# Feed-forward part: two passes over halves of the inner dimension, six token tiles a block, GpSimd's work on VectorE

## The chip, the cores and the metric

One core of a Trainium2 chip. A core has TensorE (PE, the matmuls), VectorE (DVE), ScalarE (ACT), GpSimd (POOL) and SyncE (SP), which here issues the DMAs; each takes its instructions in the order in which they stand in its queue. The metric is the device time in microseconds (us), lower is better.

## The reference

Local attention feeds a soft mixture of experts, and that feeds a gated feed-forward part:

```python
x = attention(q, k, v)                    # (2304, 512), 8 heads, window 32, plain or dilated
logits = x @ phi                          # 32 slots: 8 experts x 4
d = softmax(logits over tokens); slot_input = d.T @ x
slot_out = relu(slot_input @ w1[e]) @ w2[e]      # 8 experts, inner dimension 1024
x = softmax(logits over slots) @ slot_out        # c @ slot_out
h = x @ w_in                              # (2304, 2048)
g = h * sigmoid(h)                        # silu
out = g @ w_out                           # (2304, 512)
```

w_in (512 x 2048) and w_out (2048 x 512) arrive as 64-bit floats, all else as 32-bit ones.

## The kernel before

The kernel is a list of operations: `op(name, engine, cost, deps, fn)` records one, with an estimated cost and with what it must come after. `list_schedule` (line 885) puts all of them in one order: each engine takes, of those that are ready by the estimated times, the one with the longest estimated way to the end behind it, with small bonuses by kind (`PRIO`). The engines' queues follow that order, so the order within a queue is fixed beforehand. `mm` (line 78) records every matmul, so all matmuls have line 79.

The first 160 us are attention, the two softmaxes and the experts, with their weights streamed. Then comes the feed-forward part, from line 503 on. Because c has 32 columns only, A = slot_out @ w_in (32 x 2048) is formed first and h = c @ A afterwards. The inner dimension of 2048 is taken in 16 pieces of 128, called f; the 2304 tokens in 18 tiles of 128, called t. All products are exact to two parts: a value is split into a rounded high part and the rest.

For each f these are made:

- `cvi` (line 561, three DVE instructions at lines 539, 541 and 543) turns 64-bit w_in into 32-bit, `aq` (582) multiplies it into a piece of A in a PSUM bank, `ah` on ACT and `al` on DVE split that, and eight or four small ACT copies `ac` (618) put it in its place `astk`. One conversion of 512 columns is half of what two f need of w_in.
- `cvo` (568) turns one f of w_out into 32-bit, again three DVE instructions; `wh` (line 576, ACT) makes its high part, `wl` (663, GpSimd) subtracts that and leaves the rest. The four places of `wt` hold a raw w_out piece until its `wl` is done.
- `h` is the matmul of A's piece with c (transposed, in `ct`), into bank 6 or 7; ACT's silu (`si`, line 714) writes its result to `gtm`; `gh` is its high part, in the first group a second ACT pass over the bank (720), later a DVE cast (722); `gl` the rest (727), on GpSimd in the first group, on DVE later.
- `om` adds gh x wh, gh x wl and gl x wh for one f and one tile into the tile's bank: three matmuls of 512 columns.

The tokens come in five groups of 5, 4, 4, 3 and 2 tiles. The first group goes f by f, as w_in and w_out are converted, with all five tiles open in five banks; its h comes in two parts, 256 and 384 columns wide. The other groups go tile by tile, with all 16 f of a tile in a row, from g values that are kept in the places where weights had been (`ring`). Each tile's bank is copied out once (`oe`, DVE and ACT in turn) and stored. The last tile goes in two halves of 256 columns.

Of the kernel before, what the change touches and what calls it, by code (L numbers as in the profile page):

```python
# [29 lines left out]
def fused_kernel(ctx: ExitStack, tc: tile.TileContext, a: dict):  # L30
# [5 lines left out]
    # ---- constants and small persistent tiles  # L36
# [26 lines left out]
    # ---- places that several tiles use one after the other: a new tile in a place begins once  # L63
    # every use of the one before it has been emitted
# [16 lines left out]
    # ---- a list of operations, each on one engine, with what it must come after; they are  # L81
    # put in an order by a small list scheduler, and emitted in that order
# [11 lines left out]
    # ================= attention =================  # L94
# [52 lines left out]
    def scores(m):  # L147
# [6 lines left out]
        # the plain heads' masks are the dilated ones' second block over and over, but for the first  # L154
# [136 lines left out]
    # ---- dispatch: softmax over tokens, kept as a running one over the four batches  # L291
# [6 lines left out]
    # what the batches so far have summed to is kept relative to their maximum  # L298
# [23 lines left out]
    # ---- combine: softmax over slots, transposed, in two exact parts  # L322
# [74 lines left out]
    # ---- token sums of the four batches put together, scaled, transposed  # L397
# [30 lines left out]
    # ---- experts, their weights streamed  # L428
# [78 lines left out]
    WIS = (("w10", "", ""), ("w11",), ("xk",), ("xq",), ("w10", "w11"), ("xk", "xq"))  # L507
    WIG = ((0, 2, 3, 4), (0, 4), (0, 4), (0, 4), (0, 2, 4), (0, 2, 4))
    WIC = ((0, 2), (2, 4), (4, 6), (6, 8), (8, 12), (12, 16))
    WIF = (("w12", 0), ("w12", 1024), ("xu", 0), ("xu", 1024), ("w12", 0), ("xu", 0))  # L510
    WOS = ("w13", "w14", "xp")

    def wi(q, k):
        w = 256 * (WIC[q][1] - WIC[q][0])
        if q == 0:
            return reg("wi0", w * WIG[0][k], w * (WIG[0][k + 1] - WIG[0][k]))
        return reg(f"wi{q}.{k}", 0, 2048)

# [13 lines left out]
    # the 32-bit form of a 64-bit float: sign and top exponent bit, the low seven bits of the  # L532
    # exponent and the mantissa's top 23
# [20 lines left out]
    def wif(q):  # L554
        place, o = WIF[q]
        key = f"wif{q - (o > 0)}"
        if key not in tiles:
            new(place, key)
        return reg(key, o, 512 * (WIC[q][1] - WIC[q][0]))

    def cvi(q, k, i):
        if q == 0:
            o, n = (0, 512, 768)[k], (512, 256, 256)[k]
            conv(wi(0, k), wif(0)[:, o:o + n], i)
        else:
            conv(wi(q, k // 2)[:, 1024 * (k % 2):1024 * (k % 2) + 1024], wif(q)[:, 512 * k:512 * k + 512], i)
# [6 lines left out]
    def whc(f):  # L573
        if f % 2 == 0:
            new(f"w{f // 2}", f"ws{f // 2}", F32R)
        act.copy(out=wh(f), in_=wt(f))  # L576

    def arow(q):
        f0, f1 = WIC[q]
        return slice(32 * (f0 % 4), 32 * (f0 % 4 + f1 - f0))  # L580

    def aq(q):
        f0, f1 = WIC[q]
        n = f1 - f0
        w = wif(q).rearrange("p (g f) -> p g f", g=4)
        for g in range(4):
            for s in range(n):
                r = 32 * ((f0 + s) % 4)
                mm(bank[4][r:r + 32, 384:512], sot[:, 32 * g:32 * g + 32], w[:, g, 128 * s:128 * s + 128], g == 0, g == 3)

    def ahc(q):
        act.copy(out=aqh[arow(q)], in_=bank[4][arow(q), 384:512])

    def alc(q):
        dve.tensor_tensor(out=aql[arow(q)], in0=bank[4][arow(q), 384:512], in1=aqh[arow(q)], op=ALU.subtract)
# [418 lines left out]
```

## Time and profile before

| | us |
|---|---|
| median of 3 runs | 416.8 (414.83 to 419.25) |
| the profiled execution, span | 416.7 |
| PE busy | 373.5 |
| DVE busy | 250.6 |
| ACT busy | 168.9 |
| GpSimd busy | 101.4 |

The span runs from the first to the last instruction. Busy times are sums over the whole span, so an engine that fills one stage and rests in another shows a middling share. A digit of the slices is the busy share of a fortieth of the span (10.4 us) in tenths.

### The profile page before, as it was taken

The numbers are of one execution on the slowest core, as the hardware profiler recorded it, in microseconds if no ns is written. First come the engines' busy times: TensorE is split into PE (matmuls) and PEld (weight loads), VectorE is DVE, ScalarE is ACT, GpSimd is POOL, SyncE is SP. The second block draws the span as 40 slices with busy tenths as digits, with TensorE's granted clock in tenths as the row PEclk, the third lists the DMA queues.
The fourth block names the chain that finished last, engine by engine and source line by source line (L and its number), as shares of the span: only waits on it lengthen the run. The fifth ranks groups of instructions, "written<-read, shape, count | busy, mean of one in ns | idle before, by whom it ended". The sixth has DMA issues, their size and how long they took to land.

```text
span 416.7 us, 8042 instructions
## 1 busy us (share of the span) xinstructions
PE 373.5 (90%) x3042; PEld 287.9 (69%) x3042; DVE 250.6 (60%) x614; ACT 168.9 (41%) x596; POOL 101.4 (24%) x118
## 2 busy tenths in 40 slices
PE   4797987998989998778786999999999999999997
PEld 3676766877862345546564678888888888888886
DVE  5888988888652028999999807900294004900730
ACT  2585655675521125455555856400252002400510
POOL 4314221221222013576928881000000000000000
PEclk9898998999999999989969899999999999999999
DMA  8999999997998999967320002020001000010000
GB/s 229 265 338 330 288 302 296 312 324 240 353 352 301 386 387 397 401 253 272 131 102 0 1 2 76 2 76 25 27 0 51 27 8 18 2 50 27 25 25 27
DMA packets 33080, 70.04 MB, mean 168 GB/s; under 512 B 2705, under 2 KB 3217, under 8 KB 33041
## 3 DMA queue, kind: packets, MB, share of 16 engines
q1 hardware_dynamic: 33040, 69.53, 49.8%
q8 instruction: 24, 0.39, 0.4%
q14 instruction: 16, 0.12, 0.1%
HBM read 64.80 MB, written 4.72 MB: 167 GB/s over the span
## 4 chain that ended last, share of the span: by engine, by line
PE 55%; DVE 25%; DMA 10%; ACT 3%; issue 2%; SPq 2%; POOL 1%; POOLq 0%; ACTq 0%; DVEq 0%
PE bank L79 55%; DMA w_w2.15_1839<-in_w 3%; ACT xp_pq L178 2%; DVE xu_wif L541 2%; DMA w_w1.2_342<-in_w 2%; DMA xp_pq<-in_q 2%; DVE xu_wif L543 2%; DVE xt_wt L541 2%; DVE xt_wt L543 2%; DVE w_wif L541 2%; DVE xt_pt L203 2%; DVE xt_pt L202 2%; DMA xv_v<-in_v 2%; DVE xt_pt L205 2%; DMA xk_k<-in_k 1%
## 5 line engine op out<-in xcount | busy, mean ns | idle before, releaser
L79 PE MATMUL bank<-w_ws,w_g 128*128 128x512 f32 (+1 forms) x318 | 75.1, 379 | 0.0
L714 ACT ACTIVATE xv_gtm<-bank 128x256 f32<-128x256 f32 (+2 forms) x96 | 46.7, 492 | 54.8 <-PE bank L79 52.7
L79 PEld LDWEIGHTS bank<-w_ws,w_g 128*128 128x128 f32 x318 | 56.8, 188 | 11.1
L178 ACT ACTIVATE xp_pq<-bank,stats 128x64 f32<-128x64 f32 x144 | 43.7, 337 | 29.7 <-DVE stats L170 23.8
L79 PE MATMUL bank<-w_ws,x_gz 128*128 128x512 f32 x165 | 46.6, 420 | 1.1 <-POOL w_ws L663 0.4
L191 POOL TENSOR_TENSOR xp_pq<-xp_pq,stats 128x320 f32<-128x320 f32 (+1 forms) x32 | 21.7, 678 | 74.8 <-ACT xp_pq L178 31.7
L79 PEld LDWEIGHTS bank<-w_ws,x_gz 128*128 128x128 f32 x165 | 32.2, 201 | 10.0 <-POOL x_gz L727 1.4
L663 POOL TENSOR_TENSOR w_ws<-xt_wt,w_ws 128x512 fp32r<-128x512 f32 x16 | 27.4, 1715 | 23.5 <-ACT w_ws L576 17.8
L79 PE MATMUL bank<-xk_k,xq_qp 128*64 128x64 f32 x576 | 25.8, 239 | 7.9 <-DVE xq_qp L144 7.8
L178 ACT ACTIVATION_READ_ACCUMULATOR xp_pq<-bank,stats 128x1 f32 x144 | 32.8, 228 | 0.0
L79 PE MATMUL bank<-ct_ct,w_astk 128*128 128x256 f32 (+2 forms) x96 | 31.9, 342 | 0.6 <-ACT w_astk L622 0.4
L809 DVE COPY w_ost<-bank 128x512 f32<-128x512 f32 x9 | 6.1, 686 | 41.7 <-PE bank L79 41.7
L79 PEld LDWEIGHTS bank<-xk_k,xq_qp 128*64 128x64 f32 x576 | 21.2, 148 | 14.2 <-DVE xq_qp L144 10.0
L79 PE MATMUL bank<-ip,xu_v2x 128*128 128x160 f32 x160 | 28.3, 316 | 1.7 <-DVE lg L262 1.5
L79 PE MATMUL bank<-xt_pt,xv_v 128*64 128x96 f32 (+1 forms) x396 | 23.6, 274 | 5.2 <-POOL xp_pq L191 2.1
L808 ACT COPY w_ost<-bank 128x512 f32<-128x512 f32 x8 | 4.7, 588 | 55.0 <-PE bank L79 54.8
L79 PEld LDWEIGHTS bank<-xt_pt,xv_v 128*64 128x64 f32 x396 | 21.2, 158 | 8.0 <-POOL xp_pq L191 2.2
L727 POOL TENSOR_TENSOR x_gz<-xv_gtm,x_gz 128x256 fp32r<-128x256 f32 (+1 forms) x22 | 25.2, 1161 | 1.9 <-ACT xv_gtm L714 1.9
L79 PEld LDWEIGHTS bank<-ip,xu_v2x 128*128 128x128 f32 x160 | 22.4, 189 | 4.2 <-DVE lg L262 1.6
L722 DVE CAST w_g<-xv_gtm 128x512 fp32r<-128x512 f32 (+2 forms) x30 | 11.7, 390 | 20.2 <-ACT xv_gtm L714 19.8
L79 PEld LDWEIGHTS bank<-ct_ct,w_astk 128*128 128x128 f32 x96 | 18.0, 189 | 5.8 <-ACT w_astk L622 1.3
L79 PE MATMUL bank<-w_ws,w_gy 128*128 128x512 f32 x75 | 21.1, 420 | 0.9 <-POOL w_gy L727 0.9
(222 smaller groups left out, 652.8 us busy)
## 6 DMA issues: line engine op xcount, KB each, us to landing
w_wo<-in_w_out SPq DMA_DIRECT2D x5, 1024.0 KB, 8.4
xp_pq<-in_q SPq DMA_DIRECT2D x16, 288.0 KB, 7.2
xk_k<-in_k SPq DMA_DIRECT2D x16, 288.0 KB, 7.0
out<-w_ost SPq DMA_DIRECT2D x17, 256.0 KB, 2.0
xv_v<-in_v SPq DMA_DIRECT2D x44, 72.0 KB, 6.2
xp_wo<-in_w_out SPq DMA_DIRECT2D x2, 1024.0 KB, 9.6
xu_v2x<-in_v SPq DMA_DIRECT2D x20, 72.0 KB, 5.9
w_w1.0_136<-in_w SPq DMA_DIRECT2D x1, 1024.0 KB, 8.5
```

The costliest lines, as they stand in the source:

```text
L79: pe.matmul(out, lhsT=lhsT, rhs=rhs, start=start, stop=stop, skip_group_check=True)
L178: act.activation(out=preg(n)[:, j0 + i, :], in_=bank[m % 3][:, 64 * i:64 * i + 64], func=ACTF.Exp, bias=nmx[:, r, i:i + 1], accum_out=sums ...
L191: pool.tensor_tensor(out=p, in0=p, in1=rinv[:, m % 4, 0:nj].rearrange("p (j o) -> p j o", o=1).to_broadcast([128, nj, 64]), op=ALU.mult)
L202: dve.transpose(out=t[0:64, j0:j1, 32:64], in_=p[64:128, j0:j1, 0:32])
L203: dve.transpose(out=t[64:128, j0:j1, 32:64], in_=p[64:128, j0:j1, 32:64])
L205: dve.transpose(out=t[64:128, ja - 1:j1 - 1, 64:96], in_=p[0:64, ja:j1, 0:32])
L541: dve.scalar_tensor_tensor(out=out, in0=hi, scalar=0xC0000000, in1=out, op0=ALU.bitwise_and, op1=ALU.bitwise_or)
L543: dve.scalar_tensor_tensor(out=out, in0=lo, scalar=29, in1=out, op0=ALU.logical_shift_right, op1=ALU.bitwise_or)
L663: lambda f=f: (pool if f >= WLD else dve).tensor_tensor(out=wl(f), in0=wt(f), in1=wh(f), op=ALU.subtract))
L714: act.activation(out=gtm(G, f, s), in_=hb(G, f, s), func=ACTF.Silu)
L722: dve.tensor_copy(out, gtm(G, f, s))
L727: (pool if eng == "POOL" else dve).tensor_tensor(out=gl[:, c], in0=gtm(G, f, s), in1=gh[:, c], op=ALU.subtract)
```

## The change

The tokens now come in three groups of six tiles, and the inner dimension in two passes: blocks 0 to 2 take f = 0 to 7 for the three groups, blocks 3 to 5 take f = 8 to 15 for the same groups. Every block goes f by f, with six tiles open in six banks (0, 1, 2, 3, 5 and 4); `h` always is 384 columns wide, two of them for one f. After a block of the first pass the six banks are copied to `part` (ACT and DVE in turn), in places where weights had been. After a block of the second pass DVE adds `part` to the bank (`oe`), writes to `ost` (four places) and the tile is stored; the last tile's addition and store go in two halves. g values have three places, each used again after three f.

`wl` and the first block's `gl` stand on DVE instead of GpSimd. w_in comes in eight equal pieces of two f, instead of four such and four halves of a double one; the pieces of A go to columns 384 to 511 of banks 6 and 7, beside `h`, instead of banks 4 and 3. The order of the loads changes from the fifth w_in piece on.

```diff
-    WIC = ((0, 2), (2, 4), (4, 6), (6, 8), (8, 12), (12, 16))
+    WIS = ("w10", "w11", "xk", "xq", "w10", "w11", "w10", "w11")
...
+    def apl(i):
+        return bank[6 + i % 2][:, 384:512]
     def aq(q):
...
-                mm(bank[4][r:r + 32, 384:512], sot[:, 32 * g:32 * g + 32], w[:, g, 128 * s:128 * s + 128], g == 0, g == 3)
+                mm(apl(q)[r:r + 32], sot[:, 32 * g:32 * g + 32], w[:, g, 128 * s:128 * s + 128], g == 0, g == 3)
...
-        we = "POOL" if f >= WLD else "DVE"
-        op(f"wl{f}", we, 1.23 if f >= WLD else .6, [f"wh{f}"],
-           lambda f=f: (pool if f >= WLD else dve).tensor_tensor(out=wl(f), in0=wt(f), in1=wh(f), op=ALU.subtract))
+        op(f"wl{f}", "DVE", .6, [f"wh{f}"],
+           lambda f=f: dve.tensor_tensor(out=wl(f), in0=wt(f), in1=wh(f), op=ALU.subtract))
-    groups = [(0, 5), (5, 4), (9, 4), (13, 3), (16, 2)]
-    units = [(0, f, s) for f in range(16) for s in range(2)] + [(G, f, 0) for G in range(1, len(groups)) for f in range(16)]
+    NB, NTL, FH = 6, 6, 8
+    SW = 64 * NTL
+    units = [(B_, f, s) for B_ in range(NB) for f in range(FH * (B_ // 3), FH * (B_ // 3) + FH) for s in range(2)]
...
+    def gslot(G, f):
+        return (G * FH + f % FH) % 3
...
-        return bank[6 + uid[G, f, s] % 2][:, 0:c1 - c0]
+    def hb(u):
+        return bank[6 + u[2]][:, 0:SW]
+    def hmm(u):
+        G, f, s = u
+        mm(hb(u), asl(f), reg("ct", (G % 3) * 2 * SW + s * SW, SW), True, True)
...
+    def glc(u):
+        dve.tensor_tensor(out=ghalf(u, 1), in0=gtm(u), in1=ghalf(u, 0), op=ALU.subtract)
...
+    PLS = ("xk", "xq", "xu", "xp", "w13")
+    PFREE = ("cvi2.1", "cvi3.1", "aq3", "cvo11", "cvo13")
+    def part(i):
+        if i % 4 == 0 and f"part{i // 4}" not in tiles:
+            new(PLS[i // 4], f"part{i // 4}")
+        return reg(f"part{i // 4}", (i % 4) * 512, 512)
...
+        pb = units[uid[u] - 6] if uid[u] >= 6 else None
+        gd += [f"om{pb[0]}.{NTL // 2 * s + NTL // 2 - 1}.{pb[1]}"] if pb else ["sotm1", "L2.15"]
+        op(f"gh{x}", "ACT" if G == 0 else "DVE", .05 + SW * .00083 if G == 0 else .07 + SW * .00052, gd, lambda u=u: ghc(u))
+        op(f"gl{x}", "DVE", .07 + SW * .00104, [f"gh{x}", f"si{x}"], lambda u=u: glc(u))
+    for G in range(NB):
+        f0 = FH * (G // 3)
+        for f in range(f0, f0 + FH):
+            for t in range(NTL):
...
+                if f == f0:
+                    d += [f"oe{G-1}.{t}"] if G else [("L1.15", "cbs3.1", "sotm1", "soe1", "cbs3.0", "sote")[t], "he1", "hr1", "sotm1"]
...
+                    op(f"om{G}.{t}.{f}", "PE", 3 * .216, d, lambda G=G, t=t, f=f: om(G, t, f, (0, 1)))
+        for t in range(NTL):
+            i = (G % 3) * NTL + t
+            if G < 3:
+                d = [f"om{G}.{t}.{f0 + FH - 1}", PFREE[i // 4]]
+                if i % 2:
+                    op(f"oe{G}.{t}", "ACT", .5, d, lambda i=i, t=t: act.copy(out=part(i), in_=obank(t)))
+                else:
+                    op(f"oe{G}.{t}", "DVE", .6, d, lambda i=i, t=t: dve.tensor_copy(part(i), obank(t)))
+                continue
+            n = 2 if i == NT // 128 - 1 else 1
+            for k in range(n):
+                c = slice(512 // n * k, 512 // n * (k + 1))
+                x = f"{G}.{t}" + (f".{k}" if k else "")
+                op(f"oe{x}", "DVE", .6 / n, [f"om{G}.{t}.{f0 + FH - 1}", f"do{i-4}" if i >= 4 else "cvi6.1", f"oe{G}.{t}" if k else None],
+                   lambda i=i, t=t, c=c: dve.tensor_tensor(out=ost(i)[:, c], in0=obank(t)[:, c], in1=part(i)[:, c], op=ALU.add))
+                op(f"do{i + k}", "SP", .4, [f"oe{x}"], lambda i=i, c=c, out=out: sp.dma_start(out=out[:, c], in_=ost(i)[:, c]))
...
-    loads += ["lwo2", "lwi2.0", "lwo4", "lwi3.0", "lwo6", "lwi4.0", "lwi4.1", "lwo8", "lwo10", "lwi5.0", "lwi5.1", "lwo12", "lwo14"]
+    loads += ["lwo2", "lwi2.0", "lwo4", "lwi3.0", "lwo6", "lwi4.0", "lwo8", "lwi5.0", "lwo10", "lwi6.0", "lwo12", "lwi7.0", "lwo14"]
```

## Rows read from the trace of the kernel before

**Rows 1.** the page: busy us by engine, then DVE in 40 slices, tenths

```profile
PE 373.5 (90%) x3042; PEld 287.9 (69%) x3042; DVE 250.6 (60%) x614; ACT 168.9 (41%) x596; POOL 101.4 (24%) x118
...
DVE  5888988888652028999999807900294004900730
```

**Rows 2.** the chain that ended last, in order of time: start us, us, what

```profile
244.33 169.30 PE bank L79 x792
413.65 0.37 ACT w_ost L803
```

**Rows 3.** windows: us; busy us of PE, PEld, DVE, ACT, POOL; clock, DMA share, GB/s

```profile
208.40:214.00 5.60, 4.11 (x23) 2.70 (x24) 5.57 (x12) 1.83 (x6) 0.01 (x1) 0.50 0.01 3
218.00:227.50 9.50, 7.03 (x51) 4.99 (x49) 9.50 (x9) 6.57 (x18) 9.33 (x7) 1.00 0.00 0
163.70:244.30 80.60, 63.05 (x336) 45.68 (x328) 74.98 (x92) 48.48 (x134) 56.12 (x42) 0.92 0.44 165
```

**Rows 4.** waits from 163 to 252 us: who waited for whom, us, times, longest

```profile
PE bank L79 <- DVE xu_wif L543: 8.1, 7, 2.0
PE bank L79 <- DVE w_wif L543: 7.0, 4, 3.0
```

**Rows 5.** timeline of GpSimd: start us, us, what, [idle before]

```profile
214.32 1.40 POOL L663 TENSOR_TENSOR w_ws<-xt_wt,w_ws 128x512 fp32r<-128x512 f32 x1 [5.91 <-ACT w_ws L576]
...
223.20 1.71 POOL L663 TENSOR_TENSOR w_ws<-xt_wt,w_ws 128x512 fp32r<-128x512 f32 x1
```

**Rows 6.** timeline of VectorE: start us, us, what

```profile
209.48 0.41 DVE L539 TENSOR_SCALAR xt_wt<-w_wo 128x512 uint32<-128x512 uint32 x1
209.82 0.68 DVE L543 SCALAR_TENSOR_TENSOR w_wif<-w_wi4.1_2141,w_wif 128x512 uint32<-128x512 uint32 x1
210.42 0.68 DVE L541 SCALAR_TENSOR_TENSOR xt_wt<-w_wo,xt_wt 128x512 uint32<-128x512 uint32 x1
...
223.71 1.75 DVE L543 SCALAR_TENSOR_TENSOR xu_wif<-xk_wi5.0_2241,xu_wif 128x512 uint32<-128x512 uint32 x1
```

**Rows 7.** windows of VectorE alone: us, busy us (xcount), TensorE clock, DMA share, GB/s

```profile
160.70:240.30 79.60, 77.52 (x98) 0.91 0.49 182
```

**Rows 8.** timeline of TensorE: start us, us, what

```profile
163.79 0.56 PE L79 MATMUL bank<-ct_ct,w_astk 128*128 128x256 f32 x2
...
238.63 0.34 PE L79 MATMUL bank<-ct_ct,w_astk 128*128 128x384 f32 x1
238.81 2.92 PE L79 MATMUL bank<-w_ws,w_gy 128*128 128x512 f32 x12
...
269.08 6.98 PE L79 MATMUL bank<-w_ws,w_g 128*128 128x512 f32 x30
...
280.09 6.97 PE L79 MATMUL bank<-w_ws,w_g 128*128 128x512 f32 x30
```

**Rows 9.** groups of one line and form: xcount | busy us, mean ns | idle before

```profile
L727 DVE TENSOR_TENSOR w_g<-xv_gtm,w_g 128x512 fp32r<-128x512 f32 x16 | 11.1, 693 | 0.5
L714 ACT ACTIVATE xv_gtm<-bank 128x384 f32<-128x384 f32 x26 | 12.8, 492 | 12.3 <-PE bank L79 11.1 <-DVE w_g L722 1.2
L809 DVE COPY w_ost<-bank 128x512 f32<-128x512 f32 x9 | 6.1, 686 | 41.7 <-PE bank L79 41.7
L622 ACT CAST w_astk<-chi 32x128 fp32r<-32x128 f32 x17 | 5.0, 297 | 0.3
...
L576 ACT CAST w_ws<-xt_wt 128x512 fp32r<-128x512 f32 x16 | 9.9, 621 | 2.3 <-DVE xt_wt L543 2.0
```

**Rows 10.** timeline of VectorE, 384 columns wide: start us, us, what

```profile
349.09 0.36 DVE L722 CAST xu_g<-xv_gtm 128x384 fp32r<-128x384 f32 x1 [17.41 <-ACT xv_gtm L714]
349.49 0.56 DVE L727 TENSOR_TENSOR xu_g<-xv_gtm,xu_g 128x384 fp32r<-128x384 f32 x1
349.96 0.36 DVE L722 CAST xu_g<-xv_gtm 128x384 fp32r<-128x384 f32 x1
```

**Rows 11.** the page, DMA issues: KB each, median us from issue to landing

```profile
out<-w_ost SPq DMA_DIRECT2D x17, 256.0 KB, 2.0
```

More of the change, by code (lines that the diff above doesn't have):

```diff
@@ L573, in whc @@
     def whc(f):
-        if f % 2 == 0:
+        if f"ws{f // 2}" not in tiles:
             new(f"w{f // 2}", f"ws{f // 2}", F32R)
@@ L690, in gnew, with gtm @@
-    def gnew(G, f, s):
-        e = (G - 1) * 16 + f
-        if G == 0 and f == s == 0:
+        key, o = (("gz", 0), ("gz", 4 * SW), ("gy", 0))[gslot(G, f)]
+        return reg(key, o, 2 * SW), reg(key, o + 2 * SW, 2 * SW)
+    def gnew(u):
+        if uid[u] == 0:
             new("x", "gz", F32R)
             new("w8", "gy", F32R)
-        if G > 0 and e % 2 == 0:
-            new(ring[(e // 2) % len(ring)], f"g{e // 2}", F32R)
-    def gtm(G, f, s):
+    def gtm(u):
         if "gtm" not in tiles:
@@ L744, in ost @@
     def ost(i):
         if "ost" not in tiles:
-            new("w8", "ost")
+            new("w10", "ost")
         return reg("ost", (i % 4) * 512, 512)
@@ L758, in fused_kernel @@
-        if G == 0:
-            p = [f"gl0.{f-3}.{s}"] if f >= 3 else ["L2.4"]
-        elif uid[u] < 36:
-            p = [f"gl0.{min(13 + f, 15)}.{r}" for r in range(2)]
-        else:
-            p = [f"gl{uname(units[uid[u] - 4])}"]
-        op(f"si{x}", "ACT", .05 + w * .00083, [f"h{x}", "pre"] + p, lambda u=u: silu(*u))
-        gd = [f"h{x}", "pre"] if G == 0 else [f"si{x}"]
-        if G == 0:
-            gd += [f"om0.{part0[s][1]-1}.{f-3}"] if f >= 3 else ["sotm1", "L2.15"]
-        else:
-            e = (G - 1) * 16 + f - f % 2
-            if e >= NR:
-                pG, pf = divmod(e - NR, 16)
-                gd += [f"om{pG+1}.{groups[pG+1][1]-1}.{pf+1}"]
-            else:
-                gd += [rfree[ring[e // 2]]]
@@ new lines, in fused_kernel @@
+        op(f"h{x}", "PE", .19, ([f"ac{f}.{r}" for r in range(4)] if f > 1 else [("al0", "alr0")[f]]) + p, lambda u=u: hmm(u))
+        op(f"si{x}", "ACT", .05 + SW * .00083, [f"h{x}", "pre", f"gl{back(3)}" if back(3) else "L2.4"], lambda u=u: silu(u))
+        gd = [f"h{x}", "pre"] if G == 0 else [f"si{x}"]
+        pb = units[uid[u] - 6] if uid[u] >= 6 else None
+        gd += [f"om{pb[0]}.{NTL // 2 * s + NTL // 2 - 1}.{pb[1]}"] if pb else ["sotm1", "L2.15"]
+        op(f"gh{x}", "ACT" if G == 0 else "DVE", .05 + SW * .00083 if G == 0 else .07 + SW * .00052, gd, lambda u=u: ghc(u))
@@ L871 @@
 EST = {}
-ACE = ("ACT", "ACT", "ACT", "ACT")
 L2W = 8
```

202 lines of the change are left out of this document (68 added, 134 removed).

## The prediction

> **The bound.** I read the page's busy times and slices first, then the windows by stage, the chain that ended last, the waits, and last the timelines of VectorE (DVE), GpSimd (POOL) and TensorE (PE). The page gives PE 373.5 of 416.7 us [rows 1]; that average hides two stages. DVE's slices 16 to 23 (156 to 240 us) stand at 8 or 9 tenths [rows 1], its later ones mostly low. From 244.33 us to 413.63 PE runs without a gap, 169.30 us of the chain [rows 2]: there only fewer PE columns or a shorter tail could gain. Ahead of it, from 163.70 to 244.30, PE is busy 63.05 of 80.60 us, DVE 74.98 and POOL 56.12 [rows 3]. This is where the feed-forward part starts while w_in and w_out are still being converted, and 15.1 us of PE's waiting there is for the third conversion step, L543 [rows 4]. So DVE sets that stage.
>
> Why DVE is so busy is read in the timelines. With POOL idle (before 214.32, 5.91 us of it [rows 5]) the three steps of a 512-wide conversion start 0.34, 0.60 and 0.60 us after one another [rows 6], so 1.54 us in all. While POOL subtracts (from 223.20) the same third step takes 1.75 us [rows 5, 6]. Between 160.70 and 240.30 DVE is busy 77.52 us [rows 7] with 30 such conversions (16 for w_out, 14 for w_in) and some 2 us else; clean they would be 30 x 1.54 = 46.2. About 29 us are lost beside POOL. DMA is not the cause: between 218.00 and 227.50 nothing moves (DMA share 0.00) and POOL is busy 9.33 of 9.50 us, with the slow steps in it [rows 3, 6].
>
> **PE's debt.** The first h product starts at 163.79 [rows 8]. One token tile of 48 matmuls takes 280.09 - 269.08 = 11.01 us, 0.2294 a matmul [rows 8]; 18 tiles are 198.2 us. A 384-wide h takes 0.18 us [rows 8]; the new kernel has 96, 17.3 us. The pieces of A after the first (seven, eight small matmuls each) I put at 0.4 us, an estimate: the 128 columns of each are a quarter of a 512-wide matmul, 8 x 0.057 = 0.46 at most, and side by side in their columns less. 2.8 us. Before and after have the same matmul columns, so with no gap PE would end at 163.8 + 198.2 + 17.3 + 2.8 = 382.1. Before ended at 413.6: 31.5 us are lost, nearly all ahead of 244.33, and no rearrangement can win more.
>
> **The change.** *GpSimd's subtractions go to DVE.* 16 wl (512 wide): the same form on DVE takes 0.693 us [rows 9], less the 0.09 by which neighbours overlap (0.56 long, 0.47 from start to start [rows 10]): 0.60. The gl of block 0: 16 of 384 columns, 0.47 each. Together 9.6 + 7.5 = 17 us more DVE work, and the 29 us lost beside POOL go.
>
> *Six tiles a block, eight f in a pass.* One f of block 0 now is 18 matmuls and two h: 18 x 0.2294 + 0.36 = 4.49 us of PE (before, 15 matmuls). Two f, which share one piece of A, are 9.0 + 0.4 = 9.4 us. DVE owes for the same two: two w_in and two w_out conversions 6.16, two wl 1.2, four gl 1.9, one al 0.25 = 9.5 us. The two engines are level. Before, five tiles gave some 7.5 + 0.4 us of PE for two f, against conversions that took over half as long again. And only 8 of 16 f are needed in block 0. ScalarE (ACT) owes for two f eight silu passes of at most 0.49, two wh casts of 0.62 and eight copies of 0.30 [rows 9]: 7.6 of 9.4 us, so it isn't next.
>
> *The other eight f* need 16 x 1.54 + 4.8 + 1 = 30.4 us of DVE in blocks 1 and 2, beside 32 pairs of gh and gl at 0.87 (0.40 + 0.47 [rows 10]) = 27.8 and six of the copies out of PSUM at 0.69 = 4.1: 62.3 of the 2 x 35.9 = 71.8 us that PE needs. They are hidden by PE; were they not, up to 30 us would stand in front of block 3.
>
> *Partial sums.* 18 copies out of PSUM and 18 additions instead of 18 copies. A bank is wanted again five tiles (5 x 0.69 = 3.4 us) after its tile ended and a copy takes 0.69 [rows 9], so I cost them at nothing; additions are 12.4 us of DVE in blocks 3 to 5, where gh and gl take 41.8 of 107.7. Without that cover each boundary would show one copy, 0.7 x 5 = 3.5 us. No row shows an addition from PSUM and SBUF: bounds 0.56 (the 384-wide subtraction [rows 10]) and 1.2 (a copy from PSUM and a subtraction, 0.69 each, less their overlap); I take 0.69, which both 512-wide forms take [rows 9]. At 1.2 the additions would be 21.6 us of DVE, still inside, and the end 1 us later.
>
> *Loads* keep their order up to the w_out piece for f = 6 and 7; what follows is wanted after block 2. SP's queue holds nothing else by then, so nothing is late.
>
> *The end.* Six tiles end within 3.4 us instead of one. The store ring has four places, so the fifth addition waits for the first store: its tile ends 3.4 us before PE does, plus 0.69 and 0.33 for the issue (estimate from the issues' length) and 2.0 to land [rows 11], 0.4 us ahead of PE's end. Then that addition, two halves of the sixth (1.0 us more) and one store like the last one before: 3.9 us after PE's end, against 416.7 - 413.6 = 3.1 before. Bounds 3.1 (all as before) and 7 (two waits on a store's 2.0 us added).
>
> *What is left of the gaps in block 0.* Start: 1 us, since om needs wl and gl of f = 0, now one after another on DVE. Each later pair of f has the chain from the last conversion through A, its split, four to eight ACT copies of 0.30, h, silu and gl: about 0.5 + 0.3 + 0.3 + 1.2 + 0.2 + 0.5 + 0.5 = 3.5 us. Below: 0, if conversions run a pair ahead. Above: 3 x 3.5 = 10.5. DVE has no spare time to run ahead, but PE still has the second f of a pair to do; I take 2 us a pair, 6 us. One drop of the clock: in the window 208.40 to 214.00, after PE's waits, the granted clock is 0.50 (1.2 GHz) with 4.11 us busy [rows 3], so 2 us lost; bounds 0 and three such, 6. Pieces of A now stand in the banks of h (6 and 7; before in bank 4 and one in 3): 0.3 us each if little waits, 2 us; bounds below in the rivals. Together 11.
>
> Sum: 382.1 + 11 + 3.9 = 397. The profiled execution's span is 416.7 and the median 416.8, so I add nothing. The runs spread from 414.83 to 419.25; 1% is about what a measurement of this kernel can tell from no change.
>
> **A rule.** A reader of a bank takes 0.49 us per silu pass of 384 columns [rows 9], and each h is read twice in block 0. The Trainium skill, "PSUM — Partial Sum Buffer", section "PSUM bank collisions raise a hardware error", says to guard PSUM by bank and quadrant, not by address. By that, a piece of A would wait until ACT has read the h that shares its bank, and the next h until the piece is read; nothing in this trace has a piece and an h in one bank, so no run here shows it yet. By that page the sum would be that of rival 2, 406, and by address alone 397.
>
> **Rivals.**
>
> 1. *Gapless* (0.15): DVE keeps ahead, clock stays up, 2 us of gaps: 382.1 + 2 + 3.9 = 388. For it: DVE's 9.5 is level with PE's 9.4. Against: level means no reserve.
>
> 2. *The chain through A is exposed* (0.27): A in h's banks is serialised. A piece then waits for two silu passes (about 0.9) and the next h for the two reads of the piece (0.3 + 0.3 and hops, 0.7): 7 x 1.6 = 11 us instead of 2: 406; with the whole 10.5 for the chain 411. For it: PE takes its queue in order, so such a wait stops the om behind it. Against: h can be three f ahead.
>
> 3. *The second half's conversions come first* (0.05), the case that ends slower. DVE's order is fixed beforehand; 30.4 us of conversions for f of 8 and up are independent of block 0. If they are queued ahead of its gl, PE stands still for them and blocks 1 to 5 can't give it back, as PE fills them. All of it: 397 + 30 = 427. It is slower than before once 20 us of the 30 are ahead. Against: the order goes by the longest way to the end, and a gl of block 0 has five more blocks behind it, these conversions three.
>
> 4. *The slow conversions were not POOL's doing* (0.03). Then about 1 us stays on each: 14 more in block 0, and blocks 1 and 2 need 62 + 16 = 78 against 72, 6 more: 417, no change. Against: the slow steps stand beside POOL with DMA at rest, the clean ones where POOL rests [rows 3, 5, 6].
>
> **The numbers.** Forecast 0.50 for 393 to 402. The range 388 to 409 takes in the gapless case and most of rival 2, and leaves out rivals 3 and 4 and the top of 2. The list order of the attention part may shift by a few us either way with the new tail; that lies inside it. Faster by over 1% (below 412.6): 0.91 (forecast, rival 1 and nearly all of 2); within 1%: 0.05 (rival 4, the ends of 2 and 3); slower: 0.04 (the rest of 3).
>
> **To look for.** Right: POOL idle after the combine softmax; conversions at 0.41 and 0.69 us throughout; DVE over 90% busy from 161 to about 205, PE over 85% there; PE without gaps after block 0; the start of the feed-forward part near 163.8 and PE's end near 393. Wrong: steps of 1.2 us and more with POOL idle (rival 4); PE waiting for ACT at the pieces of A (rival 2); conversions of later w_in columns on DVE while PE waits for gl (rival 3); PE idle at block boundaries, waiting for a copy or an addition.

## The result and the profile after

The changed kernel takes 399.67 us (median of four runs, 398.71 to 400.83), the kernel before 417.69 us in the runs beside it. The ratio is 0.9585 with a 95% interval of 0.9547 to 0.9624, so 4.15% faster, about 17 us by the ratio (18.0 between the two medians). The forecast was 397 in a range of 388 to 409. The profiled execution spans 399.1 us.

The page of the changed kernel: busy time of each engine, then VectorE (DVE), GpSimd (POOL) and the clock granted to TensorE (PE) in 40 slices.

```profile
PE 369.2 (93%) x2994; PEld 286.4 (72%) x2994; DVE 264.4 (66%) x699; ACT 164.1 (41%) x581; POOL 39.1 (10%) x70
...
DVE  5887998788764014989899998433873373465435
...
POOL 5324212121124001000000000000000000000000
PEclk9998999899899999999999999999999999999999
```

Against [rows 1], POOL has lost 62 us of work and does nothing from slice 17 on (160 us; a slice is 10.0 us here, and slices are counted from 1). DVE has gained only 14 us although 85 instructions more stand on it (699 against 614): 16 wl, 32 gl, 16 gh and 19 additions among them. Its slices 17 to 25 (160 to 249 us) are still at 8 or 9 tenths; behind them it is at 3 to 8, where it was mostly idle before.

The chain that ended last, in order of time (start us, us, what):

```profile
185.60 208.10 PE bank L79 x970
393.72 0.70 DVE w_ost L779
```

PE's unbroken stretch now starts at 185.60; in [rows 2] it started at 244.33. The windows (us; busy us of PE, PEld, DVE, ACT, POOL; granted clock, DMA share, GB/s), first block 0, then the rest of the feed-forward part, then both:

```profile
163.80:206.00 42.20, 38.16 (x199) 29.41 (x196) 38.25 (x76) 26.58 (x69) 0.00 (x0) 1.00 0.58 215
206.00:395.04 189.04, 189.04 (x879) 154.66 (x877) 114.54 (x237) 58.47 (x132) 0.00 (x0) 1.00 0.12 43
163.80:395.04 231.24, 227.21 (x1076) 184.08 (x1072) 152.79 (x312) 85.06 (x201) 0.00 (x0) 1.00 0.20 74
```

In block 0 PE and DVE are both 90% busy, and the clock stays at 1.00. From 206 us on PE has not one gap: 189.04 us busy of 189.04. What [rows 4] listed as 15.1 us of waiting for the third conversion step is now, for the whole feed-forward part (who waited for whom, us, times, longest):

```profile
PE bank L79 <- ACT xv_gtm L697: 4.0, 3, 1.5
```

DVE's timeline shows the conversion steps at their clean price, 0.42 and 0.68 us long and 0.34 and 0.60 apart, in the middle of block 0; in [rows 6] the third step took 1.75 there:

```profile
189.91 0.42 DVE L540 TENSOR_SCALAR xt_wt<-xp_wo 128x512 uint32<-128x512 uint32 x1
190.24 0.68 DVE L544 SCALAR_TENSOR_TENSOR xu_wif<-xq_wi,xu_wif 128x512 uint32<-128x512 uint32 x1
190.84 0.68 DVE L542 SCALAR_TENSOR_TENSOR xt_wt<-xp_wo,xt_wt 128x512 uint32<-128x512 uint32 x1
191.45 0.42 DVE L540 TENSOR_SCALAR xt_wt<-w_wo 128x512 uint32<-128x512 uint32 x1
```

PE's timeline has its three waits and the pieces of A (lines of 16 records, 128 wide):

```profile
163.80 0.90 PE L79 MATMUL bank<-ct_ct,w_astk 128*128 128x384 f32 x2
165.99 0.44 PE L79 MATMUL bank<-ct_ct,w_astk 128*128 128x384 f32 x1 [1.29 <-ACT xv_gtm L697]
...
172.81 1.07 PE L79 MATMUL bank<-w_wif,lg 128*32 128x128 f32 x16
...
177.77 1.07 PE L79 MATMUL bank<-xu_wif,lg 128*32 128x128 f32 x16 [1.24 <-ACT xv_gtm L697]
...
185.60 0.45 PE L79 MATMUL bank<-ct_ct,w_astk 128*128 128x384 f32 x1 [1.50 <-ACT xv_gtm L697]
```

The first h starts at 163.80, where it started before [rows 8]. Everything that was won lies behind it.

### The profile page after: what moved, and what is told of

Same layout as the page of the kernel before. It is cut to its first block, busy times and chain, and to the rows that moved or that the text cites. A ratio compares the mean times of both kernels' runs of the same rounds, so it can differ in the third digit from the quotient of the medians.

```text
span 399.1 us, 7930 instructions
## 1 busy us (share of the span) xinstructions
PE 369.2 (93%) x2994; PEld 286.4 (72%) x2994; DVE 264.4 (66%) x699; ACT 164.1 (41%) x581; POOL 39.1 (10%) x70
## 4 chain that ended last, share of the span: by engine, by line
PE 68%; DVE 11%; DMA 10%; ACT 6%; SPq 2%; issue 2%; POOL 1%; DVEq 0%; ACTq 0%; POOLq 0%
PE bank L79 68%; DMA w_w2.15_1839<-in_w 3%; ACT xp_pq L178 3%; DMA xp_pq<-in_q 2%; DMA w_w1.0_136<-in_w 2%; DVE xt_pt L203 2%; DVE xt_pt L202 2%; DVE xt_pt L205 2%; DMA w_w1.1_260<-in_w 1%; DVE xt_pt L201 1%; DVE xq_qp L144 1%; DMA xk_k<-in_k 1%; DVE stats L170 1%; POOL xp_pq L191 1%; ACT w_astk L619 1%
## 5 line engine op out<-in xcount | busy, mean ns | idle before, releaser
L79 PE MATMUL bank<-w_ws,x_gz 128*128 128x512 f32 x576 | 145.4, 396 | 0.0
L79 PEld LDWEIGHTS bank<-w_ws,x_gz 128*128 128x128 f32 x576 | 107.3, 188 | 23.7 <-issue 1.0
L697 ACT ACTIVATE xv_gtm<-bank 128x384 f32<-128x384 f32 x96 | 47.0, 492 | 115.3 <-PE bank L79 114.4
L79 PE MATMUL bank<-w_ws,w_gy 128*128 128x512 f32 x288 | 71.1, 392 | 0.0
L79 PEld LDWEIGHTS bank<-w_ws,w_gy 128*128 128x128 f32 x288 | 53.6, 188 | 11.0 <-issue 0.2
L704 DVE CAST x_gz<-xv_gtm 128x384 fp32r<-128x384 f32 x52 | 18.7, 359 | 42.0 <-ACT xv_gtm L697 41.5
L707 DVE TENSOR_TENSOR x_gz<-xv_gtm,x_gz 128x384 fp32r<-128x384 f32 x64 | 35.5, 557 | 5.8 <-ACT xv_gtm L697 1.2
L79 PE MATMUL bank<-ct_ct,w_astk 128*128 128x384 f32 x96 | 32.9, 346 | 2.8 <-ACT xv_gtm L697 2.8
L144 DVE TENSOR_SCALAR xq_qp<-xp_pq 64x576 f32<-64x576 f32 x32 | 17.3, 540 | 5.3 <-DMA xp_pq<-in_q 5.0
L707 DVE TENSOR_TENSOR w_gy<-xv_gtm,w_gy 128x384 fp32r<-128x384 f32 x32 | 17.8, 557 | 2.6 <-ACT xv_gtm L697 0.7
(193 smaller groups left out, 397.1 us busy)
```

Source lines behind the costliest of these rows:

```text
L79: pe.matmul(out, lhsT=lhsT, rhs=rhs, start=start, stop=stop, skip_group_check=True)
L144: dve.tensor_scalar(out=dst[64 * z:64 * z + 64, :, z, :], in0=src[64 * z:64 * z + 64], scalar1=D ** -0.5, scalar2=None, op0=ALU.mult)
L697: act.activation(out=gtm(u), in_=hb(u), func=ACTF.Silu)
L704: dve.tensor_copy(ghalf(u, 0), gtm(u))
L707: dve.tensor_tensor(out=ghalf(u, 1), in0=gtm(u), in1=ghalf(u, 0), op=ALU.subtract)
```

## The experiments

The theory that was tested: the gain is the work taken off POOL, because POOL's subtractions slowed DVE by more than they relieved it, and DVE set block 0; six tiles and two passes add a part that is smaller. The rivals: the two passes bring the gain and the move to DVE is incidental; DVE's slow steps had another cause; the gaps that are left come from silu and the shared banks, not from DVE.

The profiled executions start the feed-forward part at different times (159.96 to 163.80 us in those where nothing new stands ahead of it). In the chain of the changed kernel a transfer of expert weights, 146.41 to 158.01, ends just ahead of that start. So beside the times this table gives the feed-forward part alone, from the first h to PE's end, from one profiled execution of each; idle is the length less PE's busy time, the tail is the span less PE's end.

| kernel | us, median | ratio to before, interval | length | PE busy | PE idle | tail |
|---|---|---|---|---|---|---|
| before | 416.6 to 417.7 | 1 | 249.82 | 232.24 | 17.58 | 3.1 |
| passes and six tiles, POOL kept | 415.10 | 0.9961 (0.9942, 0.9980) | 247.17 | 233.54 | 13.63 | 4.0 |
| offload alone | 402.99 | 0.9669 (0.9644, 0.9694) | 235.68 | 227.09 | 8.59 | 3.1 |
| offload and six tiles, one pass | 401.73 | 0.9643 (0.9601, 0.9685) | 234.25 | 228.06 | 6.19 | 4.0 |
| changed | 399.67 | 0.9585 (0.9547, 0.9624) | 231.24 | 227.21 | 4.03 | 4.1 |

### The parts of the change

**The subtractions on DVE, nothing else**, in the kernel before:

```diff
-WLD = 0
-GLD = 0
+WLD = 16
+GLD = 16
```

> The kernel before with one part of the change alone: the 32 subtractions wl and gl of the feed-forward part go from GpSimd to VectorE, while the loop stays one pass in token groups of five, six and five tiles. Contention theory: VectorE's work in the stage of 77.5 us loses the excess that it paid beside GpSimd (29 us estimated) and gains the 16 wl of 0.68 us and the 16 half gl of 0.4 to 0.55 us, net about 6 to 10 us less; but the five-tile group still puts 16 conversions in as many steps of 4.1 us, so VectorE stays the slower one there. Expected 405 to 411 us, the rest of the change's gain lying in the two passes. Rival, that the whole gain comes from the offload and the two passes only save stores: 398 to 402 us. Rival, that VectorE does not slow beside GpSimd: at or above 417 us.

Measured 402.99 us, ratio 0.9669 (0.9644 to 0.9694): 13.8 of the 17 us by the ratios. That lies between the two ranges: more than I expected of the offload, less than the whole. The expectation also describes the kernel wrongly: its groups stay at 5, 4, 4, 3 and 2 tiles, and 48 subtractions move (16 wl and 32 gl, two for each f), not 32. The window of its feed-forward part and the page's busy times:

```profile
162.37:398.05 235.68, 227.09 (x1124) 183.40 (x1120) 133.88 (x277) 88.51 (x215) 0.00 (x0) 1.00 0.20 77
```

```profile
PE 369.2 (92%) x3042; PEld 286.1 (71%) x3042; DVE 245.3 (61%) x662; ACT 167.6 (42%) x596; POOL 38.8 (10%) x70
```

DVE's total *fell* from 250.6 [rows 1] to 245.3 with 48 more instructions on it. The 16 wl and 32 half gl that it took over are 10.8 and 15.6 us of its rows, so without relief it would stand at 277.0: beside POOL it had paid 31.7 us for nothing. PE's busy time fell by 5.1 us too, at the same matmuls: the granted clock of the feed-forward part is 1.00, against 0.97 before, where [rows 3] shows 0.50 after PE's waits. Idle PE time fell by 9.0. The prediction had one drop of the clock at 2 us; the 405 to 411 expected here names no price for it.

A second way in which POOL could have cost time is that wl and gl took longer there, and PE waited for them. By the waits of the kernel before, from 163 us on, PE's waits that carry POOL's name are 0.9, 0.4 and 0.4 us, 1.7 of some 17.5. So that is the small part.

**The passes and the six-tile blocks, with the work back on POOL**, in the changed kernel:

```diff
-        op(f"wl{f}", "DVE", ...  dve.tensor_tensor(out=wl(f), ...
+        op(f"wl{f}", "POOL", ... pool.tensor_tensor(out=wl(f), ...
...
-        dve.tensor_tensor(out=ghalf(u, 1), ...
+        (dve if u[0] else pool).tensor_tensor(out=ghalf(u, 1), ...
...
```

> The changed kernel with its 16 wl and the first block's 16 gl put back on GpSimd; the two passes and the six-tile blocks stay. Contention theory: VectorE loses 16 times 0.68 and 16 times 0.56 us, some 20 us of work, but its conversions beside a busy GpSimd go from 1.6 us to about 3 to 4 us each, so the first block is no longer done in 8 steps of 4.5 us. Expected 405 to 409 us, with VectorE's rows of 0.34 and 0.60 us at 0.4 to 1.7 again. Rival, that the GpSimd part of the change is worth nothing once conversions are spread over two passes: 398 to 402 us.

Measured 415.10 us, ratio 0.9961 (0.9942 to 0.9980): 1.6 us better than before, and much worse than I expected. The page's busy times, and then, from the timelines of DVE and POOL, two conversion steps in one row (1.28 us together in the changed kernel) and the wl beside them:

```profile
PE 373.8 (90%) x2994; PEld 287.6 (70%) x2994; DVE 274.0 (66%) x667; ACT 163.2 (39%) x581; POOL 84.6 (20%) x102
```

```profile
197.54 3.21 DVE L542 SCALAR_TENSOR_TENSOR w_wif<-w_wi,w_wif 128x512 uint32<-128x512 uint32 x2
...
197.28 1.50 POOL L658 TENSOR_TENSOR w_ws<-xt_wt,w_ws 128x512 fp32r<-128x512 f32 x1 [0.28 <-ACT w_ws L576]
```

With 32 instructions fewer than in the changed kernel (16 x 0.683 + 16 x 0.557 = 19.8 us) DVE should be at 244.6; it is at 274.0. The 32 subtractions on POOL cost DVE 29.4 us, 0.92 each on the mean of the 512-wide and the 384-wide ones, where doing them itself costs 0.60 (in the timeline of the changed kernel) and 0.47 [rows 10] from start to start. So the two passes and the six tiles without the offload are worth 0.4%.

**One pass**, with the offload and six tiles:

```diff
-    NB, NTL, FH = 6, 6, 8
+    NB, NTL, FH = 3, 6, 16
...
-            if G < 3:
+            if G < 0:
...
-   dve.tensor_tensor(out=ost(i)[:, c], in0=obank(t)[:, c], in1=part(i)[:, c], op=ALU.add)
+   dve.tensor_copy(ost(i)[:, c], obank(t)[:, c])
```

> The changed kernel with one pass of 16 inner tiles over three blocks of six, six and four token tiles, so no partial sums are kept or added; everything else, VectorE's subtractions too, stays. It differs from the changed kernel by the two passes alone. My theory: VectorE has to carry 16 conversions with their wl and gl in the first block at 4.5 us a step, which the changed kernel's first block does for 8 of them with 4 us of gaps in TensorE's row; eight more such steps add about as much again, and the adds and copies saved cost TensorE nothing. Expected 401 to 406 us. Rival, that the second pass is what frees VectorE and a one-pass first block falls behind step by step: 410 us or more. Rival, that partial sums cost as much as they bring: 396 to 399 us.

Measured 401.73 us, ratio 0.9643 (0.9601 to 0.9685), as expected. (Its three blocks are six tiles each, not six, six and four.) The interval overlaps that of the changed kernel, so the times alone don't settle what the second pass is worth (2 us by the medians). The traces are sharper:

```profile
159.96:394.21 234.25, 228.06 (x1076) 183.98 (x1072) 142.57 (x287) 85.92 (x208) 0.00 (x0) 1.00 0.21 74
```

```profile
PE bank L79 <- ACT xv_gtm L697: 6.0, 6, 1.5
PE bank L79 <- DVE w_ws L658: 0.2, 1, 0.2
```

The feed-forward part is 3.0 us longer than in the changed kernel: 2.2 us of idle time more, in seven waits instead of three, and 0.8 of busy time. Twice as many conversions in the first block bring half as much idle time again, no more: with six tiles and a silent POOL, DVE is nearly level with PE anyway.

### What POOL does to DVE

Four kernels put idle work on POOL in the changed kernel: 32 operations on the 512 columns of hsb, which nobody reads any more, one behind each wh and one behind each silu of block 0. Nothing waits for them.

```diff
+    def zdup():
+        pool.tensor_tensor(out=hsb, in0=hsb, in1=hsb, op=ALU.subtract)
...
+        op(f"zw{f}", "POOL", 1.3, [f"wh{f}", "ht1"], zdup)
...
+        if G == 0:
+            op(f"zg{x}", "POOL", 1.0, [f"si{x}", "ht1"], zdup)
```

> The changed kernel with 32 idle subtractions on GpSimd whose result nobody reads: 512 columns of an attention buffer that is no longer used, minus itself, one behind each wh and one behind each silu of the first block. Nothing waits for them. Contention theory: they take some 30 to 40 us of the first block's time on GpSimd, and VectorE's conversions beside them stretch from 0.34, 0.60, 0.60 us towards 1.7 us as in the kernel before; VectorE falls behind by 10 to 20 us: 408 to 418 us. Rival, that VectorE's slow conversions in the kernel before had another cause than GpSimd at work (the data they read, the transfers): 398 to 402 us.

Measured 423.43 us, ratio 1.0175 (1.0139 to 1.0210): slower than the kernel before, and above what I expected. DVE's timeline in block 0, with POOL's subtractions in an unbroken row beside it:

```profile
166.36 0.29 DVE L615 TENSOR_TENSOR w_astk<-bank,w_astk 64x128 fp32r<-64x128 f32 x1
...
173.21 1.26 DVE L540 TENSOR_SCALAR w_wif<-w_wi 128x512 uint32<-128x512 uint32 x1
174.39 1.52 DVE L661 TENSOR_TENSOR w_ws<-xt_wt,w_ws 128x512 fp32r<-128x512 f32 x1
175.84 1.39 DVE L711 TENSOR_TENSOR x_gz<-xv_gtm,x_gz 128x384 fp32r<-128x384 f32 x1
...
159.69 37.47 POOL L655 TENSOR_TENSOR hsb<-hsb 128x512 f32<-128x512 f32 x28
```

Clean, the three forms take 0.42, 0.68 and 0.55 us. Each of these rows is longer by 0.84, whatever its own length. The small one that reads a bank (L615) takes 0.29 as without POOL.

The same with `pool.memset(hsb, 0.0)`, which reads nothing:

> As the run with idle GpSimd subtractions, but each is a memset of the same 512 columns, which writes and reads nothing. If any work of GpSimd slows VectorE, the same 408 to 418 us less what a memset is shorter; if it is GpSimd's reading of two operands, near 400 us. I take the first as likelier only by its share of time: about 404 us.

Measured 400.22 us, ratio 0.9605 (0.9572 to 0.9638), no different from the changed kernel: the 404 that I took as likelier was wrong, and the other reading held. Here only L540 is slowed, the form with a single operand in SBUF, which takes 0.42 us clean for its 512 columns, 0.34 from start to start:

```profile
172.59 0.82 DVE L540 TENSOR_SCALAR xt_wt<-w_wo 128x512 uint32<-128x512 uint32 x1
...
174.07 0.67 DVE L542 SCALAR_TENSOR_TENSOR xt_wt<-w_wo,xt_wt 128x512 uint32<-128x512 uint32 x1
...
158.08 20.04 POOL L655 MEMSET hsb<- 128x512 f32 x32
```

With `pool.tensor_copy(hsb, hsb)`, one operand read:

> The run with idle GpSimd work once more, now with a copy of the same 512 columns onto themselves: one operand read, one written, where the subtraction reads two and the memset none. In the measured pair the subtraction added 24.2 us of VectorE time for 39.8 us of GpSimd (0.61 us for each), the memset 1.0 us for 18.2 us. If the slowing goes with the number of operands read, half of 0.61 for each us of GpSimd: some 8 us more on VectorE and 403 to 409 us. If only a second operand brings it: 399 to 401 us. If any read brings all of it: 412 us or more.

Measured 408.94 us, ratio 0.9816 (0.9777 to 0.9855), at the upper end of the first expectation. Each of the DVE instructions below takes 0.41 more, half of what the subtraction costs:

```profile
169.63 0.83 DVE L540 TENSOR_SCALAR w_wif<-w_wi 128x512 uint32<-128x512 uint32 x1
170.38 1.09 DVE L661 TENSOR_TENSOR w_ws<-xt_wt,w_ws 128x512 fp32r<-128x512 f32 x1
171.39 0.96 DVE L711 TENSOR_TENSOR x_gz<-xv_gtm,x_gz 128x384 fp32r<-128x384 f32 x1
...
159.38 26.49 POOL L655 COPY hsb<-hsb 128x512 f32<-128x512 f32 x29
```

And the subtraction cut into two of 256 columns:

> The run with idle GpSimd subtractions, each cut into two of 256 columns: the same GpSimd work in twice as many instructions. In the run with 512 columns each VectorE instruction with its operands in SBUF took 0.84 us more beside them whatever its own length (0.42 to 1.26, 0.55 to 1.39, 0.68 to 1.52). If VectorE waits out one GpSimd instruction at a time: half of it, about 0.42 us more for each (0.84, 0.97, 1.10), while GpSimd takes its turns twice as often, so that the sum stays near 24 us and the time at 415 to 425 us. If the surcharge is a fixed one for every VectorE instruction that meets a busy GpSimd: 0.84 us again and the rows of 1.26 and 1.52 us.

Measured 418.23 us, ratio 1.0036 (0.9997 to 1.0075). The rows are those of the first theory:

```profile
168.78 0.83 DVE L540 TENSOR_SCALAR w_wif<-w_wi 128x512 uint32<-128x512 uint32 x1
169.53 1.10 DVE L662 TENSOR_TENSOR w_ws<-xt_wt,w_ws 128x512 fp32r<-128x512 f32 x1
170.55 0.96 DVE L712 TENSOR_TENSOR x_gz<-xv_gtm,x_gz 128x384 fp32r<-128x384 f32 x1
...
156.02 57.90 POOL L656 TENSOR_TENSOR hsb<-hsb 128x256 f32<-128x256 f32 x64
```

The four together, DVE's excess being its busy time on the page less the 264.4 us of the changed kernel:

| POOL's idle work | POOL us | more for each DVE instruction that meets it | DVE's excess |
|---|---|---|---|
| 32 subtractions, 512 wide | 39.8 | 0.84 | 24.2 |
| 64 subtractions, 256 wide | 57.9 | 0.41 | 22.9 |
| 32 copies, 512 wide | 26.7 | 0.41 | 10.4 |
| 32 memsets, 512 wide | 18.3 | 0.4 for L540, 0 for the others | 1.0 |

So the two engines take turns: a DVE instruction waits out the turn of one POOL instruction, here about 0.41 us for each 512 columns of an operand that POOL reads. The excess fits one wait for nearly every POOL instruction: 24.2 / 0.84 = 29 of 32, 22.9 / 0.41 = 56 of 64, 10.4 / 0.41 = 25 of 32. That POOL waits in its turn is inferred, from the 256-wide subtractions, which take 0.90 us each (57.90 for 64 in a row) where the 512-wide take 1.34 (37.47 for 28) and not twice as long. Cutting POOL's work into shorter instructions shortens each wait and multiplies them; the sum stays.

The price of 0.84 is that of the idle subtraction, which has one tile as both operands and as its result. Beside the kernel's own wl, from two tiles into a third, the step in [rows 6] took 1.75 instead of 0.68 us, so 1.07 more. What makes the difference was not tested.

The Trainium skill, "SBUF — State Buffer", section "SBUF: two separate sides", describes a pair of SBUF ports that DVE and POOL share by an exclusive lock, held for a whole instruction, and wanted by a DVE instruction in a two-port mode or with two SBUF inputs, the latter only against a POOL instruction that reads SBUF. These rows agree with it down to the memset, which slows L540 from 0.42 to 0.82 us and leaves the two-input forms at 0.67; how long POOL holds the lock they show only by DVE's waits.

### What bounds block 0 now

**More on DVE**: the high half of g in block 0 as a DVE copy instead of a second Silu on ScalarE (ACT).

```diff
-        if u[0] == 0:
-            act.activation(out=ghalf(u, 0), in_=hb(u), func=ACTF.Silu)
-        else:
-            dve.tensor_copy(ghalf(u, 0), gtm(u))
+        dve.tensor_copy(ghalf(u, 0), gtm(u))
...
-        op(f"gh{x}", "ACT" if G == 0 else "DVE", ...
+        op(f"gh{x}", "DVE", ...
```

> The changed kernel with the first block's 16 high halves of g made by VectorE from the silu's result, as in the later blocks, and no longer by a second Silu on ScalarE: 16 operations of about 0.36 to 0.40 us more on VectorE while the conversions run, 6 us in all, 16 of 0.56 us less on ScalarE. If VectorE's order sets TensorE's few gaps in the first block: 3 to 6 us slower, 402 to 406 us. If VectorE has slack there and the gaps come from the silu and the banks: 398 to 401 us, or a little less.

Measured 402.42 us, ratio 0.9651 (0.9634 to 0.9669), about 2.7 us slower than the changed kernel. Its order came out differently. PE's waits are now both named after DVE, one of 0.5 us and one of 4.91, and behind the long one stands a piece of A at a granted clock of 0.50 (1.92 us instead of 1.07).

```profile
169.36 1.92 PE L79 MATMUL bank<-w_wif,lg 128*32 128x128 f32 x16 [4.91 <-DVE w_wif L544]
```

**Less on DVE**: the middle conversion step left out.

```diff
-        op(f"{b}{k}", "DVE", .34 if half else .6, [f"{a}{k}"], lambda: fn(1))
-        op(f"{kind}{k}", "DVE", .34 if half else .6, [f"{b}{k}"], lambda: fn(2))
+        op(f"{kind}{k}", "DVE", .34 if half else .6, [f"{a}{k}"], lambda: fn(2))
```

> The changed kernel without the second of the three VectorE steps of each weight conversion of the feed-forward part; it leaves out part of the computation, so the converted weights are not the reference's, and the time says only what 0.6 us less for each conversion is worth. If VectorE's order is behind TensorE's gaps in the first block: those 4 us shrink to 1 us or less, 395.5 to 397.5 us. If the gaps come from the silu and the shared banks: 398.5 to 401 us, as without the edit.

Measured 396.12 us, ratio 0.9503 (0.9477 to 0.9529), 3.5 us faster, as expected. Here too the queues' order is made anew, so single waits can't be set against each other, only the sums. PE idles 1.03 us in the whole feed-forward part:

```profile
163.00:390.74 227.74, 226.71 (x1076) 184.24 (x1072) 135.16 (x282) 84.83 (x200) 0.00 (x0) 1.00 0.20 75
```

```profile
PE bank L79 <- ACT x_gz L701: 0.5, 1, 0.5
PE bank L79 <- ACT w_astk L619: 0.5, 1, 0.5
```

The waits of the changed kernel carry the name of silu, yet a faster DVE removes them: a wait is put down to what came last. At 177.77 the silu that reads the bank ended at 177.72 and the last conversion step that the piece of A needs at 177.70. So this wait can't be put on the bank alone, and DVE is what the two runs move it by.

ScalarE's part stays open. From 173.99 to 185.60 us of the changed kernel, the stretch with the last two of PE's three waits, ACT is busy 11.17 of 11.61 us, DVE 10.20 and PE 8.87. The chain that ended last runs on ACT there nearly without a break from 179.25 to 185.55, in copies of A, silu passes and a cast, and ends in the silu that the h at 185.60 waits for:

```profile
182.01 0.49 ACT xv_gtm L697
183.77 0.62 ACT w_ws L576
184.39 0.77 ACT x_gz L702 x2
```

Over all of block 0 ACT is busy only 26.58 of 42.20 us, as the prediction's "isn't next" has it. The run with more on DVE took 16 passes off ACT and was slower, so ACT isn't the only limit; a kernel that relieves ACT and leaves DVE as it is was not run.

### The tail

**The last three inner tiles of the last block, tile by tile**, so that the six sums end further apart:

```diff
-        for f in range(f0, f0 + FH):
-            for t in range(NTL):
+        fts = [(f, t) for f in range(f0, f0 + FH) for t in range(NTL)]
+        if G == NB - 1:
+            fts = [(f, t) for f in range(f0, f0 + FH - 3) for t in range(NTL)] + [(f, t) for t in range(NTL) for f in range(f0 + FH - 3, f0 + FH)]
+        for f, t in fts:
...
```

> The changed kernel with the last three inner tiles of the last block taken token tile by token tile, so that the six sums end 2.1 us apart instead of 0.7 us apart. The six additions and stores of the end are then spread, and only the last addition of 0.70 us (or its two halves) and one store of 2.1 us stand behind the last matmul. TensorE's work is the same. Expected 0.7 to 2 us less than the changed kernel, 397.7 to 399 us. Rival, that the tail is the last addition and store alone however the sums end: no change, 399 to 400 us.

Measured 398.45 us, ratio 0.9577 (0.9554 to 0.9600); the interval lies within that of the changed kernel. DVE's timeline shows the additions spread as meant:

```profile
388.48 0.69 DVE L782 TENSOR_TENSOR w_ost<-bank,xp_part 128x512 f32<-128x512 f32 x1 [1.40 <-PE bank L79]
390.57 0.69 DVE L782 TENSOR_TENSOR w_ost<-bank,w_part 128x512 f32<-128x512 f32 x1 [1.39 <-PE bank L79]
392.65 0.76 DVE L782 TENSOR_TENSOR w_ost<-bank,w_part 128x256 f32<-128x256 f32 x2 [1.39 <-PE bank L79]
```

The tail is 3.7 us (396.3 less 392.61) instead of 4.1. Both kernels were run side by side:

> The changed kernel itself, unaltered, on the chip and in the rounds of the kernel whose last tiles are taken one by one, as its measure: 398.5 to 401 us.

> The kernel whose last block takes its last three inner tiles token tile by token tile, again, beside the changed kernel on the same chip. From the first pair of profiles the time from TensorE's last matmul to the end is 0.4 us shorter, and TensorE's own stretch as long: 0.2 to 0.7 us below the changed kernel of the same rounds. Rival: no difference beyond 0.2 us.

Measured 399.60 us for the changed kernel (0.9605, 0.9572 to 0.9638) and 399.35 for the spread tail (0.9587, 0.9553 to 0.9621). The profiles again give tails of 4.1 (397.1 less 393.01) and 3.7 us (398.4 less 394.74), so 0.4 us is there in the traces; by the times it is not told from nothing. TensorE's own stretch was not as long as expected: 232.89 us, at a granted clock of 0.99, against 231.24. No version that does the whole computation and clearly beats the changed kernel came out of this.

## Why the prediction was right, step by step

**DVE sets the first stage, because of POOL: right, and shown.** The offload alone brings 13.8 us by the ratio. The 29 us that I put down as lost beside POOL measured 31.7 us over the whole kernel. Rival 4, that POOL was not the cause, is dead: idle subtractions, on which nothing waits, bring the slow steps back and make the kernel slower than before.

**The price of the moved work: right.** 0.60 for a wl, 0.47 for a gl from start to start, as DVE's timeline in the changed kernel has them (a wl from 185.49 to the next start at 186.09, and 1.02 us for two gl).

**Level engines in block 0: right.** DVE 38.25 and PE 38.16 us of 42.20, 90% both. The two experiments on either side show what level means: 5.1 us more for DVE (269.5 against 264.4 busy) cost 2.7, 0.6 less for each conversion gave 3.5.

**Gaps of 11 us: too much.** There are 4.03. The start took 1.29 where I put 1, the later pairs 1.24 and 1.50 where I put 6. The clock drop (2 us) did not come: the granted clock is 1.00 throughout, with waits of 1.50 us at most; in the run with a wait of 4.91 it stood at 0.50 behind it. The bank sharing (2 us) didn't cost what rival 2 feared: one wait of 1.24 stands at a piece of A with a silu on its bank, and it went away with faster conversions. The other six pieces show no wait. The Trainium skill, "PSUM — Partial Sum Buffer", section "PSUM bank collisions raise a hardware error", says to guard by bank and quadrant, and by that the piece has to wait for that reader. The trace has that one wait which can be of this form, and the piece's last conversion step ended only 0.02 us before the silu; so the price of sharing a bank is not shown apart.

**The floor of 382.1: too low, the step that failed.** PE's busy time from the first h to the end is 227.21 us, and I had 198.2 + 17.3 + 2.8 = 218.3. The term that was mis-sized is the pieces of A. I took 0.4 us for eight small matmuls side by side; each of the eight shows as two records, and where a piece stands between two h the distance grows from 2.27 to 3.44 us (268.37 to 271.81), so 1.17 a piece and 8.2 for seven: 5.4 more.

```profile
268.37 0.34 PE L79 MATMUL bank<-ct_ct,w_astk 128*128 128x384 f32 x1
...
270.02 1.07 PE L79 MATMUL bank<-w_wif,lg 128*32 128x128 f32 x16
...
271.81 0.34 PE L79 MATMUL bank<-ct_ct,w_astk 128*128 128x384 f32 x1
```

The row was there in PE's timeline of the kernel before, a piece with 16 records and 1.23 us:

```profile
172.37 1.23 PE L79 MATMUL bank<-w_wif,lg 128*32 128x128 f32 x16 [2.99 <-DVE w_wif L543]
```

The prediction counted its columns instead and had a full-width row, 0.2294 us for 512 columns, as the measure. One f takes 4.525 us (27.15 for six from 207.32 to 234.47), not 4.49: 1.7 more over 48. The other 1.8 us were not taken apart.

So the sum came out close because two errors nearly cancelled, 8.9 too little in the floor and 7.0 too much in the gaps, and that is luck. PE ended at 395.04 instead of 393.1, and the span is 399.1 instead of 397.

One more step was set at nothing without its row. The sum is a span, and the time of a run is longer than its span, by 1.7 to 2.1 us in every run on record (400.83 against 399.1 in the profiled execution). The prediction compared the span of one execution before, 416.7, with the median of other runs, 416.8, and added nothing.

**Copies and additions of the partial sums at nothing: right.** PE runs through every block boundary, and an addition from a bank and SBUF took 0.68 to 0.70 us, the value taken.

**The tail of 3.9: right**, 4.06. The fifth addition starts at 394.54, 0.5 us ahead of PE's end, where I put 0.4. Six tiles at the end cost 1 us against before; the offload alone, whose last tiles end one by one, keeps 3.1.

**The second half's conversions hidden behind PE: right, though not all in blocks 1 and 2.** From 206 to 280 us DVE is busy 52.23 of 74.00 us, where I put 62.3 of 71.8: four of the w_in conversions come later, between 281 and 296 us. PE has no gap in either stretch, so rival 3 did not happen.

What the prediction didn't weigh is how the gain splits. It costed the two passes and the offload as one sum. Alone the passes and six tiles bring 0.4%, the offload 3.3%; after the offload the blocks of six and the second pass bring another 0.8%. So most of what the first group lacked was DVE time, and that came from POOL's silence.

## What to carry to other kernels

Work put on GpSimd to relieve VectorE is paid back in VectorE's own time when both have their operands in SBUF: here 32 subtractions of 512 and 384 columns cost VectorE 0.92 us each beside it, and 0.60 and 0.47 us to do. Before moving work there, compare the rows of one VectorE form with GpSimd busy and idle; a surcharge that is the same for short and long instructions is a wait for turns. And a sum that comes out right is to be taken apart all the same: the price of a small matmul is read from its row, not from its columns.

## What the hardware showed that was not expected

- VectorE's surcharge beside GpSimd is the turn of one GpSimd instruction, not a share of its own time: 0.84 us beside a 512-wide subtraction, 0.41 beside a 512-wide copy or a 256-wide subtraction, for VectorE instructions of 0.42, 0.55 and 0.68 us alike. A memset slows only the single-operand form, by 0.40. Beside the kernel's own 512-wide subtraction a step took 1.07 more.
- VectorE falling behind costs TensorE twice, in waits and in clock: with the idle subtractions PE needs 234.53 us for what takes 227.21 at a steady clock. The window of that run's feed-forward part has the granted clock at 0.95, and in the page's slices it falls to 6 tenths:

```profile
166.71:415.76 249.05, 234.53 (x1072) 188.45 (x1072) 170.77 (x312) 84.74 (x199) 28.73 (x23) 0.95 0.17 59
```

```profile
PEclk9899998999999998666899999999999999999999
```

- The start of the feed-forward part is not fixed: the changed kernel itself had it at 163.80 us in one profiled execution and at 161.77 in another, with 231.24 us from there to PE's end in both. Two kernels that differ in one stage are best compared from that stage's first instruction.
